# GpSimd's products with a convolution tap: tensor-scalar in place of tensor-tensor instructions

## The chip, the cores and the metric

The kernel runs on one core of a Trainium2 chip. The metric is the device time of one execution in microseconds (us). The engines are named as the profile names them: PE (TensorE's matmuls), PEld (its weight loads), DVE (VectorE), ACT (ScalarE), POOL (GpSimd) and SP (SyncE, which here only issues DMAs).

## The reference

A causal depthwise convolution of seven taps, whose taps are shared by the 24 channels of a head and made by a softmax over the taps, and then a feed-forward part with a product in the middle:

```python
w = softmax(weight)                       # [8 heads, 7 taps], float32
x_pad = 6 zero rows ahead of x            # x: [8, 3904, 192]
conv[b, s, h*24+g] = sum_k w[h, k] * x_pad[b, s+k, h*24+g]
a = conv @ w1                             # [31232, 192] @ [192, 1024]
b = conv @ w2
h = a * b @ w3                            # [1024, 1024]
out = h @ w_out                           # [1024, 192]
```

## The kernel before, in words

**The products.** w3 and w_out are multiplied once at the start (`W_sb`), so that each token needs `a`, `b`, their product and one more matmul. The tokens are two streams of 15616 (r = 0 and 1), cut into 31 rounds of 512 tokens (the last has 256); a round treats both streams. `first_product` (line 518) makes for each of eight blocks of 128 features the two factors with 64-row matmuls (L489), casts the one on ACT (L497) and multiplies it by the other on DVE (L508) into the tile `abT`. `second_product` (line 528) multiplies `abT` by `W_sb` (L540), copies to `osb` on ACT (L545) and stores it (L552).

**The groups.** Rounds go in groups of four (lines 721 to 750): the four first products, and then the eight second products. Group 0 is rounds 0 to 3. The schedule is by hand: `manual_schedule` keeps the order of the program on each engine, and each DMA queue (SP's, POOL's) goes in the order of issue.

**The convolution** must be done ahead of the rounds that use it. It is made in three ways:

- By TensorE with band matrices (`conv`, L398), for the first rounds and, in the groups 1 to 5, for the first two rounds of the second group after p (`load_alone`, `store_alone`).
- In the groups p = 1 to 6, `shared_head` (line 295) makes the last two rounds of the group after p (one short round for p = 6), eight heads on a tile `xv` with tokens along the partitions: 128 partitions with W = 8 tokens each (W = 2 for p = 6), both streams, in bf16. Heads 0 to 3 go to POOL, heads 4 to 7 to DVE. A head is W x 2 x 24 = 384 columns (96 for p = 6).
- DVE's four heads fuse multiplication and addition (L317, L320), with an accumulator in two PSUM banks that are held for the time (`held`); ACT makes their first product (L315).

**A head on POOL** is a first product into `acc` (L325), then for each of the six other taps a product into `term` (L328) and, but for the last, an addition to `acc` (L331); the last additions write bf16 into the tile `y` (L334). `acc`, `term` and the taps `wv` are float32, `xv` bf16. POOL's order in a group (lines 726 to 733) is: head 0; from p = 2 on the four loads of `load_alone` (L342); head 1; the two loads of the next `xv` (L279); heads 2 and 3; a small DMA of zeros where a sequence starts within the tile (L292). After the group's second products stands the store of `y` (L364, POOL's queue) to the array `rows` in DRAM, which waits for DVE's heads too, and on SP's queue the transposes (L471) that read `rows` into the ring `xT`, from which the first products read. The second products of group 1 and later are stored from SP's queue.

Of the kernel before, what the change touches and what calls it, by code (L numbers as in the profile page):

```python
# [11 lines left out]
ALU = mybir.AluOpType  # L12
# [4 lines left out]
def kernel(  # L17
# [14 lines left out]
    G = D // H  # L32
    DFF = moe_w1.shape[1]
    JT = DFF // 128
    PAD = K - 1

    NS = 2
# [144 lines left out]
    for p0 in (0, Q):  # L182
        nc.gpsimd.affine_select(
            out=diag[p0:p0 + Q], in_=ones[p0:p0 + Q].to_broadcast([Q, Q + PAD]),
# [25 lines left out]
    def warm(n):  # L210
# [14 lines left out]
        out=wall, in0=wall, in1=wmax.unsqueeze(2).to_broadcast([1, H, K]), op=ALU.subtract)  # L225
# [5 lines left out]
        out=wrow, in0=wall, in1=wsum.unsqueeze(2).to_broadcast([1, H, K]), op=ALU.mult)  # L231
# [38 lines left out]
    def share(v):  # L270
        R0, R1 = SHARED[v]
        t0, n = R0 * CH, min(R1 * CH, TS) - R0 * CH
        return t0, n // 128
# [21 lines left out]
    def shared_head(v, h, f):  # L295
        xv, y = shared[v]
        W = share(v)[1]
        if y is None:
            y = shared[v][1] = work.tile(
                [128, W, NP, NS, Q], BF16, tag="convo", bufs=2, name="y")  # L300
        on_vector = f is nc.vector
        if on_vector:
            acc = held[0][1][:, h % 2, 0:W * NS * G]
        else:
            acc = work.tile([128, W * NS * G], FP32, tag="acc", bufs=2, name="acc")
        flat = acc.rearrange("p (m g) -> p m g", g=G)
        by_row = acc.rearrange("p (s r g) -> p s r g", r=NS, g=G)
        tap = lambda k: wv[:, h, k:k + 1]
        xs = lambda k: xv[:, k:k + W].rearrange("p s r c -> p (s r) c")[:, :, h * G:h * G + G]
        parts, o = [], 0  # L310
        for k, c0, m in segments(h * G, G):
            parts += [(y[:, :, k, r, c0:c0 + m], r, slice(o, o + m)) for r in range(NS)]
            o += m
        if on_vector:
            nc.scalar.activation(out=flat, in_=xs(PAD), func=ACT.Copy, scale=tap(PAD))  # L315
            for k in range(PAD - 1, 0, -1):
                f.scalar_tensor_tensor(out=flat, in0=xs(k), scalar=tap(k), in1=flat,  # L317
                                       op0=ALU.mult, op1=ALU.add)
            for dst, r, cs in parts:
                f.scalar_tensor_tensor(  # L320
                    out=dst, in0=xv[:, 0:W, r, h * G + cs.start:h * G + cs.stop],
                    scalar=tap(0), in1=by_row[:, :, r, cs], op0=ALU.mult, op1=ALU.add)
            return
        wide = lambda k: tap(k).unsqueeze(2).to_broadcast([128, W * NS, G])
        f.tensor_tensor(out=flat, in0=xs(PAD), in1=wide(PAD), op=ALU.mult)  # L325
        for k in range(PAD - 1, -1, -1):
            term = work.tile([128, W * NS * G], FP32, tag="term", bufs=2, name="term")
            f.tensor_tensor(out=term.rearrange("p (m g) -> p m g", g=G), in0=xs(k),  # L328
                            in1=wide(k), op=ALU.mult)
            if k:  # L330
                f.tensor_tensor(out=acc, in0=acc, in1=term, op=ALU.add)  # L331
        term = term.rearrange("p (s r g) -> p s r g", r=NS, g=G)
        for dst, r, cs in parts:
            f.tensor_tensor(out=dst, in0=by_row[:, :, r, cs], in1=term[:, :, r, cs], op=ALU.add)  # L334
# [38 lines left out]
    def segments(c0, n):  # L373
        out = []
        while n:
            m = min(n, Q - c0 % Q)
            out.append((c0 // Q, c0 % Q, m))
            c0, n = c0 + m, n - m
        return out
# [302 lines left out]
    def put_rows(b, last):  # L682
# [7 lines left out]
        out=wv, in0=wv, in1=top.unsqueeze(2).to_broadcast([128, H, K]), op=ALU.subtract)  # L690
# [5 lines left out]
        out=wv, in0=wv, in1=top.unsqueeze(2).to_broadcast([128, H, K]), op=ALU.mult)  # L696
# [16 lines left out]
    for p in SHARED:  # L713
        for i, h in ((-1, 4), (-1, 5), (1, 6), (3, 7)):
            at.setdefault((p, i), []).append((shared_head, p, h, nc.vector))
# [5 lines left out]
    for p, rounds in enumerate(groups):  # L721
        if p == 1:
            load_alone(1)
            pad_shared(1)
        if p in SHARED:
            for h in range(0, 4):
                shared_head(p, h, nc.gpsimd)
                if h == 0 and p > 1 and p in ALONE:
                    load_alone(p)
                if h == 1 and p + 1 in SHARED:  # L730
                    load_shared(p + 1)
            if p + 1 in SHARED:
                pad_shared(p + 1)
        for j, R in enumerate(rounds if p else ()):
            first_product(R)
            if R + GROUP < NR and j < 2:
                transposes(R + GROUP)
        if p in SHARED:
            free.append(free.pop(0))
            held.append(banks())  # L740
            free.insert(0, free.pop())
            run(at.get((p, -1), ()))
        for i, (R, r) in enumerate((R, r) for R in rounds for r in range(NS)):
            second_product(R, r, R == NR - 1 and r == 1, nc.sync if p else nc.gpsimd)
            run(at.get((p, i), ()))
        if p in SHARED:
            drained(held.pop()[0])
            store_shared(p)
            for R in range(*SHARED[p]):
                transposes(R)  # L750
# [30 lines left out]
```

## Time and profile before

| | |
|---|---|
| median of 3 runs | 517.45 us (516.1 to 517.6) |
| profiled execution, its own time | 515.89 us |
| its span | 514.2 us |
| granted TensorE clock | 1.00 |
| POOL's products of 384 columns (L328 and L325) | 120 x 828 ns and 20 x 847 ns |

A row of the profile's groups gives the line, the engine, the operation, out<-in by tile names with partitions x elements and type, the count, and after the bar the busy time (us), the mean of one (ns), and the idle time of the engine just before it with what ended it. A row in order of time begins with start and length in us and ends with the idle time before it in square brackets. The page's slices are 40 equal parts of the span, about 12.9 us each, with the busy share in tenths. "Landing" is the time from a DMA's issue to its completion.

### The profile page before, as it was taken

The page shows a single profiled execution, that of the slowest core. Times are in us where ns is not written, and L with a number is a line of the kernel's source. Part 1 is how long each engine was busy: PE and PEld are TensorE (multiplying, and loading weights), DVE is VectorE, ACT ScalarE, POOL GpSimd, SP SyncE. Part 2 cuts the span into 40 slices and gives each one's busy share as a digit, 9 for nine tenths or more (in the row PEclk, how much of TensorE's full clock was granted, in tenths as well). Part 3 has the DMA queues.
Part 4 walks back from the last instruction along what each step waited for, and adds up shares of the span by engine and source line. Part 5 has one row for each costly group of instructions (what it writes and reads, how often), then busy time and mean ns, then how long its engine had stood idle before and what let it go on. Part 6 is the DMA issues. An engine that isn't in the chain of part 4 may idle for free.

```text
span 514.2 us, 13632 instructions
## 1 busy us (share of the span) xinstructions
PE 508.4 (99%) x5608; PEld 339.1 (66%) x5608; DVE 401.1 (78%) x471; ACT 353.1 (69%) x469; POOL 321.4 (63%) x447
## 2 busy tenths in 40 slices
PE   8999999999999999999999999999999999999997
PEld 4555798454894458945598445985459845498587
DVE  6778723899959999499994999949999499972970
ACT  6887645777657776577765777657776577744762
POOL 8601534299999999699984999749997491000000
PEclk9999999999999999999999999999999999999999
DMA  8989999992965992787728787288842851035004
GB/s 118 155 152 127 134 216 231 207 197 54 193 193 149 137 108 94 237 146 102 95 93 248 141 104 91 93 255 134 93 51 94 259 112 32 2 102 171 6 3 155
DMA packets 137410, 67.91 MB, mean 132 GB/s; under 512 B 98899, under 2 KB 135939, under 8 KB 137283
## 3 DMA queue, kind: packets, MB, share of 16 engines
q0 software_dynamic: 48096, 26.92, 36.4%
q1 hardware_dynamic: 89105, 40.01, 32.7%
q8 instruction: 44, 0.72, 0.6%
q14 instruction: 19, 0.16, 0.1%
q10 hardware_dynamic: 146, 0.10, 0.1%
HBM read 39.60 MB, written 36.56 MB: 148 GB/s over the span
## 4 chain that ended last, share of the span: by engine, by line
PE 96%; DVE 2%; ACT 1%; issue 0%; ACTq 0%; DVEq 0%
PE pairs L489 60%; PE pairs L540 32%; PE pairs L398 2%; DVE abT L508 1%; PE pairs L575 1%; ACT asb L497 1%; PE pairs L451 1%; PE pairs L213 1%; DVE cprod L254 0%; ACT convo L419 0%; DVE convo L584 0%; ACT xT L463 0%; PE pairs L263 0%; PE pairs L615 0%; ACT osb L545 0%
## 5 line engine op out<-in xcount | busy, mean ns | idle before, releaser
L508 DVE TENSOR_TENSOR abT<-asb,pairs 128x1024 bf16<-128x1024 bf16 (+1 forms) x245 | 298.2, 1217 | 69.5 <-ACT asb L497 53.0
L489 PE MATMUL pairs<-xT,wd 64*128 64x512 bf16 (+2 forms) x3000 | 319.8, 371 | 0.7 <-DVE abT L508 0.3
L497 ACT CAST asb<-pairs 128x1024 bf16<-128x1024 f32 (+1 forms) x245 | 247.1, 1009 | 67.7 <-PE pairs L489 67.4
L489 PEld LDWEIGHTS <-wd 64*128 64x128 bf16 x3000 | 160.7, 94 | 153.6 <-issue 1.5
L540 PE MATMUL pairs<-W_sb,abT 128*128 128x192 bf16 x1952 | 165.0, 246 | 0.0
L540 PEld LDWEIGHTS <-abT 128*128 128x128 bf16 x1952 | 159.9, 98 | 5.3 <-issue 5.1
L545 ACT COPY osb<-pairs 128x384 f32<-128x384 f32 x122 | 58.6, 480 | 83.4 <-PE pairs L540 82.6
L331 POOL TENSOR_TENSOR acc<-acc,term 128x384 f32<-128x384 f32 (+1 forms) x120 | 107.3, 894 | 9.4
L328 POOL TENSOR_TENSOR term<-xv,wv 128x384 f32<-128x384 bf16 (+1 forms) x144 | 107.7, 748 | 0.5 <-DMA xv<-zeros 0.5
L317 DVE SCALAR_TENSOR_TENSOR pairs<-xv,wv,pairs 128x384 f32<-128x384 bf16 (+1 forms) x120 | 68.7, 572 | 7.2 <-ACT pairs L315 3.4
L364 POOL DMA_DIRECT2D rows<-y x6 | 3.7, 614 | 70.2 <-DVE y L320 61.3
L334 POOL TENSOR_TENSOR y<-acc,term 128x192 bf16<-128x192 f32 (+5 forms) x60 | 26.5, 467 | 1.9
L419 ACT CAST convo<-pairs 128x864 bf16<-128x864 f32 (+9 forms) x49 | 26.5, 613 | 0.2
L325 POOL TENSOR_TENSOR acc<-xv,wv 128x384 f32<-128x384 bf16 (+1 forms) x24 | 18.3, 764 | 9.7 <-DMA xv<-in_x_dram 9.6
L419 DVE CAST convo<-pairs 128x960 bf16<-128x960 f32 (+4 forms) x10 | 8.2, 858 | 17.2 <-PE pairs L398 17.2
L320 DVE SCALAR_TENSOR_TENSOR y<-xv,wv,pairs 128x192 bf16<-128x192 bf16 (+5 forms) x60 | 18.0, 351 | 1.1
L126 POOL DMA_DIRECT2D xb<-in_x_dram x20 | 13.9, 715 | 4.1 <-DMA xb<-in_x_dram 2.3
L342 POOL DMA_DIRECT2D xb<-in_x_dram x20 | 15.1, 772 | 0.0
L552 POOL DMA_DIRECT2D out_dram<-osb x8 | 6.1, 763 | 12.3 <-ACT osb L545 9.3
L279 POOL DMA_DIRECT2D xv<-in_x_dram x12 | 13.0, 1087 | 0.0
L315 ACT ACTIVATE pairs<-xv,wv 128x384 f32<-128x384 bf16 (+1 forms) x24 | 12.8, 550 | 0.0
L442 POOL DMA_DIRECT2D rows<-convo x2 | 1.1, 544 | 18.1 <-ACT convo L419 18.1
(65 smaller groups left out, 86.9 us busy)
## 6 DMA issues: line engine op xcount, KB each, us to landing
out_dram<-osb SPq DMA_DIRECT2D x52, 384.0 KB
xv<-in_x_dram POOLq DMA_DIRECT2D x10, 672.0 KB, 9.7
xb<-in_x_dram POOLq DMA_DIRECT2D x20, 216.0 KB, 7.3
rows<-y POOLq DMA_DIRECT2D x5, 768.0 KB, 5.9
out_dram<-osb POOLq DMA_DIRECT2D x8, 384.0 KB, 5.2
w3rows<-in_moe_w_dram POOLq DMA_DIRECT2D x2, 1024.0 KB, 11.8
xb<-in_x_dram POOLq DMA_DIRECT2D x8, 240.0 KB, 8.0
rows<-convo SPq DMA_DIRECT2D x6, 288.0 KB
```

The costliest lines, as they stand in the source:

```text
L317: f.scalar_tensor_tensor(out=flat, in0=xs(k), scalar=tap(k), in1=flat, op0=ALU.mult, op1=ALU.add)
L320: f.scalar_tensor_tensor(out=dst, in0=xv[:, 0:W, r, h * G + cs.start:h * G + cs.stop], scalar=tap(0), in1=by_row[:, :, r, cs], op0=ALU.mul ...
L325: f.tensor_tensor(out=flat, in0=xs(PAD), in1=wide(PAD), op=ALU.mult)
L328: f.tensor_tensor(out=term.rearrange("p (m g) -> p m g", g=G), in0=xs(k), in1=wide(k), op=ALU.mult)
L331: f.tensor_tensor(out=acc, in0=acc, in1=term, op=ALU.add)
L334: f.tensor_tensor(out=dst, in0=by_row[:, :, r, cs], in1=term[:, :, r, cs], op=ALU.add)
L419: f[e % len(f)](out=dst, in_=part)
L489: nc.tensor.matmul(p[:, r, e * n:e * n + n], wd[i][rs, k, ft * 128:(ft + 1) * 128], xT[k][rs, r0 + c0:r0 + c1], start=(k == 0), stop=(k == ...
L497: nc.scalar.copy(out=asb, in_=pa)
L508: nc.vector.tensor_tensor(out=dst, in0=asb, in1=pb, op=ALU.mult)
L540: nc.tensor.matmul(ops[:, (g - g0) * D:(g - g0) * D + D], ab[:, jt, r, g * 128:(g + 1) * 128], W_sb[:, jt, :], start=(jt == 0), stop=(jt = ...
L545: f(out=osb[:, g0:g0 + per, :].rearrange("p g d -> p (g d)"), in_=ops[:, 0:per * D])
```

## The change

In `shared_head`, for the heads that POOL makes, each product with a tap becomes a tensor-scalar instruction. Before, the tap `wv[:, h, k]`, one float32 value in each partition, was broadcast along all columns and went in as a second tensor; now it is the scalar operand of its partition, read from the same place in SBUF. Inputs, outputs, types and shapes stay, as do the additions and the number of instructions: 7 products a head, 4 heads a group, 6 groups, 168 in all.

```diff
-        wide = lambda k: tap(k).unsqueeze(2).to_broadcast([128, W * NS, G])
-        f.tensor_tensor(out=flat, in0=xs(PAD), in1=wide(PAD), op=ALU.mult)
+        f.tensor_scalar(out=flat, in0=xs(PAD), scalar1=tap(PAD), scalar2=None, op0=ALU.mult)
         for k in range(PAD - 1, -1, -1):
             term = work.tile([128, W * NS * G], FP32, tag="term", bufs=2, name="term")
-            f.tensor_tensor(out=term.rearrange("p (m g) -> p m g", g=G), in0=xs(k),
-                            in1=wide(k), op=ALU.mult)
+            f.tensor_scalar(out=term.rearrange("p (m g) -> p m g", g=G), in0=xs(k),
+                            scalar1=tap(k), scalar2=None, op0=ALU.mult)
             if k:
                 f.tensor_tensor(out=acc, in0=acc, in1=term, op=ALU.add)
```

## The prediction

> **What bounds the kernel now.** I read the page from the top: span and busy times, then the slices, to see whether one engine is full all the time or several take turns.
>
> ```profile
> span 514.2 us, 13632 instructions
> PE 508.4 (99%) x5608; PEld 339.1 (66%) x5608; DVE 401.1 (78%) x471; ACT 353.1 (69%) x469; POOL 321.4 (63%) x447
> PE   8999999999999999999999999999999999999997
> POOL 8601534299999999699984999749997491000000
> ```
>
> PE is full in every slice but the first and the last, and only 514.2 - 508.4 = 5.8 us of the span are not matmul time. POOL is nearly full from slice 9 on, that is from about 100 us, and done after about slice 34. So there are two questions: can PE be made to end earlier, and how near is POOL to holding PE up? The busy times of the six stretches in which PE works on one group of four rounds answer the first; the columns are start:end, length, and busy time (with instructions) of each engine.
>
> ```profile
> core 0: us, PE busy (x) PEld busy (x) DVE busy (x) ACT busy (x) POOL busy (x), PEclk, DMA share, GB/s
> 88.81:152.78 63.97, 63.97 (x673) 42.15 (x672) 54.49 (x62) 45.15 (x58) 52.02 (x65) 1.00 0.96 174
> 152.78:216.76 63.98, 63.98 (x674) 42.16 (x674) 54.49 (x62) 45.15 (x58) 57.97 (x73) 1.00 0.73 137
> 216.76:280.73 63.97, 63.97 (x673) 42.19 (x673) 54.49 (x62) 45.15 (x58) 53.17 (x67) 1.00 0.70 136
> 344.70:408.68 63.98, 63.98 (x674) 42.14 (x674) 54.49 (x62) 45.15 (x58) 52.02 (x71) 1.00 0.65 125
> ```
>
> PE is busy for the whole of each stretch (63.97 of 63.97), at a granted clock of 1.00. POOL has 52 to 58 us of work in 64. The waits of PE are all told in three rows:
>
> ```profile
> PE pairs L213 <- DVE ones L159: 1.1, 1, 1.1
> PE pairs L451 <- DVE convo L584: 0.4, 1, 0.4
> PE pairs L489 <- DVE abT L508: 0.3, 2, 0.2
> ```
>
> They come to 1.8 us, all of kinds that belong to the first 40 us, before POOL's first product. **PE bounds the kernel, and nothing that POOL does makes it wait.** A gain on POOL has nothing to shorten; a loss on POOL costs nothing until it is larger than POOL's slack.
>
> **The change, part by part.** It replaces the products of the four heads that POOL computes in each of the groups 1 to 6: one first product (L325) and six more (L328) per head, 28 per group, 140 of 384 columns in groups 1 to 5 and 28 of 96 columns in group 6. The additions (L331, L334) stay. Set beside each other, the instruction lists of the two kernels agree on PE, DVE, ACT and SP one by one, waits included; on POOL only the kind of these 168 instructions differs, in the same places with the same waits. So no DMA moves in its queue, no wait is added, and one number is unknown: how long a tensor-scalar instruction with its scalar in SBUF takes on POOL. No such row is in the trace. These are POOL's rows by form (busy us, mean ns):
>
> ```profile
> L331 POOL TENSOR_TENSOR acc<-acc,term 128x384 f32<-128x384 f32 x100 | 99.6, 996 | 7.8
> L328 POOL TENSOR_TENSOR term<-xv,wv 128x384 f32<-128x384 bf16 x120 | 99.4, 828 | 0.5 <-DMA xv<-zeros 0.5
> L325 POOL TENSOR_TENSOR acc<-xv,wv 128x384 f32<-128x384 bf16 x20 | 16.9, 847 | 9.6 <-DMA xv<-in_x_dram 9.6
> L328 POOL TENSOR_TENSOR term<-xv,wv 128x96 f32<-128x96 bf16 x24 | 8.3, 346 | 0.0
> L197 POOL COPY wd<-wd 64x768 bf16<-64x768 bf16 x6 | 4.8, 840 | 0.8 <-DMA wd<-in_moe_w_dram 0.8
> L183 POOL TENSOR_SCALAR_AFFINE_SELECT diag<-ones 64x70 bf16<-64x70 bf16 x2 | 0.5, 264 | 0.1
> L665 POOL COPY pace<-w3T 1x2 bf16<-1x2 bf16 x1 | 0.2, 174 | 11.6 <-DMA w3T<-w3rows 11.6
> ```
>
> The product now takes (99.4 + 16.9) / 140 = 0.831 us at 384 columns. From 96 to 384 columns it grows by 828 - 346 = 482 ns, 1.67 ns a column. The instructions that read one tensor are the copies: 174 ns at 2 columns, 840 at 768, so (840 - 174) / 766 = 0.87 ns a column, and at 384 columns 174 + 0.87 x 382 = 506 ns. That is the **lower bound**. The only row with scalar arithmetic in its name is the affine select: 264 ns for 70 columns. If all of that grew with the columns, 264 / 70 x 384 = 1448 ns: the **upper bound**. A tensor-scalar product reads one tensor as the copy does, with one operation on each element, so I take the value near the copy's, about 0.5 us, and keep both ends.
>
> *At 0.5 us:* POOL loses 140 x (0.831 - 0.506) = 45 us of work in groups 1 to 5, and some more in group 6. What becomes of it is read from POOL's order of time: start, length, instruction, idle time before it. Rows of the store that ends each group, and the first product of all:
>
> ```profile
> 102.99 0.83 POOL L325 TENSOR_TENSOR acc<-xv,wv 128x384 f32<-128x384 bf16 x1 [9.56 <-DMA xv<-in_x_dram]
> 154.36 0.59 POOL L364 DMA_DIRECT2D rows<-y  x1
> 212.96 0.63 POOL L364 DMA_DIRECT2D rows<-y  x1 [3.53 <-DVE y L320]
> 276.93 0.59 POOL L364 DMA_DIRECT2D rows<-y  x1 [8.90 <-issue]
> 340.92 0.63 POOL L364 DMA_DIRECT2D rows<-y  x1 [9.47 <-DVE y L320]
> 404.87 0.63 POOL L364 DMA_DIRECT2D rows<-y  x1 [9.82 <-DVE y L320]
> ```
>
> From group 2 on POOL waits 3.5 to 9.8 us before this store, because DVE's heads of the same tile are ready last. A faster POOL waits longer at the same place: the 45 us become idle time. Only group 1's store, which POOL itself holds up, would go out a few us earlier, as early as DVE's half allows. Its reader is the third round of the next group, as follows, and that round isn't waiting. The loads of the next tile and of the rows for TensorE's own convolution, which stand between the heads, go out up to some 5 to 10 us earlier within the group; PE doesn't wait for any DMA now, so nothing is won by it either. **Gain: 0.** Nor does DVE win or lose from its neighbour: its product takes the same time beside a busy POOL (first row, 213 to 267 us) and after POOL's last product (second row, 470 to 510 us).
>
> ```profile
> L508 DVE TENSOR_TENSOR abT<-asb,pairs 128x1024 bf16<-128x1024 bf16 x32 | 39.1, 1222 | 8.6 <-ACT asb L497 6.3
> ...
> L508 DVE TENSOR_TENSOR abT<-asb,pairs 128x1024 bf16<-128x1024 bf16 x20 | 24.4, 1222 | 10.8 <-ACT asb L497 9.4
> ```
>
> **How much slower POOL may be before PE notices.** The store of group p is read back by transposes on SP for the third and fourth round of group p+1. The first two rows are PE's first factors of groups 2 and 6; the third is SP's transposes after group 1's store, three for each round; the fourth and fifth are the landing times (last number, us) of that store and of the smallest row store.
>
> ```profile
> 152.78 41.62 PE L489 MATMUL pairs<-xT,wd 64*128 64x512 bf16 x384
> ...
> 408.68 41.62 PE L489 MATMUL pairs<-xT,wd 64*128 64x512 bf16 x384
> ...
> 158.19 8.45 SPq L471 DMA_TRANSPOSE xT<-rows  x6
> ...
> rows<-y POOLq DMA_DIRECT2D x5, 768.0 KB, 5.9
> rows<-convo POOLq DMA_DIRECT2D x1, 36.0 KB, 2.0
> ```
>
> From store to the third round's data: 158.19 - 154.36 = 3.8 us until the transposes start, 8.45 / 2 = 4.2 for three of them, and their landing, which no row gives; I bound it by 2.0 and 5.9. Together 10.1 to 13.9 us. The third round of group 2 starts at 152.78 + 41.62 / 2 = 173.6, so group 1's store may slip by 19.2 less that, 5 to 9 us. After group 1, POOL can use up its later waits: without them, the five groups take 51.4 (154.36 - 102.99), 55.1 (212.96 - 154.36 - 3.53), 55.1, 54.5 and 54.1 us, in all 270.2, so group 5's store could go out at 373.2. Its reader starts at 408.68 + 20.8 = 429.5. Allowed slip: 429.5 - 373.2 less 10.1 to 13.9 = 42 to 46 us, taken as 44. With d the added time of one product, PE waits once 140 d exceeds 44: d = 0.31 us, **a product of 1.15 us**. (Group 1 alone gives 28 d above 5 to 9, that is 0.19 to 0.33.) From there the time grows by 140 d - 44 us, since POOL then sets the pace of five groups.
>
> **Sum.** At any duration from 0.5 to 1.15 us the change is worth 0: 515.89 us, the profiled execution's own time (its span and 1.7 us around it). The median of the runs shown is 517.45, 1.56 above; on that scale my forecast is 517.4, no change.
>
> **The rivals.**
>
> *Slower: POOL becomes the bound.* One mechanism: the products take more than 1.15 us, the store of group 1 or 2 is late, PE stands before the third round of each next group. For it: no row shows the instruction; the affine select costs 3.8 ns a column against 1.67 for the product it would replace; POOL has only about a seventh of each group free; and forms do differ on POOL (996 ns for the addition, 828 for the product, same columns). Against it: it must be 38% slower than an instruction that reads two tensors. At the upper bound d = 1.448 - 0.831 = 0.617, and 140 x 0.617 - 44 = 42 us: 558 on the profile's scale, 559.6 on the median's. Halfway, at 1.30 us, it is 140 x 0.469 - 44 = 22 us: 539.
>
> *Much slower: the new form decides something anew for each column.* Then no row bounds it, and the same formula runs on: 2 us a product gives 140 x 1.17 - 44 = 120 us, 637. Nothing in the trace speaks for it but the affine select, which does make a choice per column, and stays within the bound above. The Trainium skill, "GPSIMD Engine Reference", 3.1, says that data-dependent branching costs about 12 cycles an element; with the 1.2 GHz of its section 1 that would be 384 x 12 / 1.2 = 3.84 us a product as an estimate, and some 377 us more, about 895 us. By that rule alone the change would be a disaster; the trace has no row of such a rate.
>
> *Faster.* It would need PE to end earlier, and the stretches above leave it no idle time after POOL's first product. Only the scatter of the runs (516.1 to 517.6) could show it.
>
> *The change does nothing to POOL either.* If the instruction runs at the old 0.83 us, all stays as it is: the same 517.4.
>
> **How the numbers follow.** No change, by a POOL that is quicker or up to 1.15 us a product: 0.52. POOL as the bound within the rows' bound, 519 to 560: 0.29. Beyond 560: 0.15, of which the per-column choice of the skill's size is 0.04. Faster: 0.04. About 0.3%, 1.55 us, is what a measurement of this kernel can tell from no change. So: faster 0.04, same 0.52, slower 0.44. The likeliest case alone spans 515.9 to 519.0; the range must take in the upper bound of the unknown duration and is 515.5 to 560, which leaves out the 0.15 above it and a little below.
>
> **What would show it.** Right: the products at about 0.5 us in POOL's groups, longer waits of the store for DVE's half in all of groups 1 to 5, stretches of PE still 63.97 us long and full. Wrong: a product of over 1.15 us, no wait left before the store, PE's first factor waiting for a DMA into xT at the third round of a group, and stretches as long as POOL's work in them. If the product is slow and the time still stands, my slack was too small; if it is quick and the time moves, something other than POOL's work, such as the loads that now go out earlier, is at play.

## The result, and the profile after

The changed kernel takes 532.68 us (median of 4 runs, 531.48 to 534.0), the kernel before in the same comparison 516.78 (515.91 to 517.6). The ratio is **1.0303, with a 95% interval of 1.0271 to 1.0335: slower by 3%**. The profiled execution took 531.48 us. The lines of its page that answer to those shown of before (the program has one line less, so L489 is now L488, L328 is L327, L364 is L363):

```profile
span 529.8 us, 13632 instructions
PE 513.8 (97%) x5608; PEld 343.8 (65%) x5608; DVE 401.0 (76%) x471; ACT 353.2 (67%) x469; POOL 388.0 (73%) x447
PE   8999999999999899999999989999899998999997
POOL 8501625199999999999999999999999999900000
```

POOL has grown from 321.4 to 388.0 us and has lost its gaps: from slice 9 to slice 35 it is never less than nine tenths busy. PE now has slices of 8. DVE and ACT have the same work as before (401.0 and 353.2 us busy, against 401.1 and 353.1). Next, POOL's rows by form (busy us, mean ns):

```profile
L327 POOL TENSOR_SCALAR term<-xv,wv 128x384 f32<-128x384 bf16 x120 | 149.2, 1243 | 0.0
L330 POOL TENSOR_TENSOR acc<-acc,term 128x384 f32<-128x384 f32 x100 | 99.6, 996 | 8.3
L324 POOL TENSOR_SCALAR acc<-xv,wv 128x384 f32<-128x384 bf16 x20 | 25.3, 1263 | 10.9 <-DMA xv<-in_x_dram 10.7
L327 POOL TENSOR_SCALAR term<-xv,wv 128x96 f32<-128x96 bf16 x24 | 12.5, 521 | 0.0
```

The product went from 828 to **1243 ns**; the addition stayed at 996. From 96 to 384 columns it grows by 722 ns, 2.51 ns a column against 1.67 before. In order of time a head is the better measure: from the first product of head 0 to that of head 1 it was 115.06 - 102.99 = 12.07 us, and is now 119.22 - 104.06 = 15.16. That is 3.09 us for seven products, **0.441 us each**. Now POOL's stores of the tile, group by group, with the first product of all:

```profile
104.06 1.25 POOL L324 TENSOR_SCALAR acc<-xv,wv 128x384 f32<-128x384 bf16 x1 [10.69 <-DMA xv<-in_x_dram]
...
167.82 0.60 POOL L363 DMA_DIRECT2D rows<-y  x1
...
235.02 0.64 POOL L363 DMA_DIRECT2D rows<-y  x1 [0.30 <-POOL y L333]
...
302.46 0.59 POOL L363 DMA_DIRECT2D rows<-y  x1
...
369.67 0.64 POOL L363 DMA_DIRECT2D rows<-y  x1 [0.31 <-POOL y L333]
...
436.47 0.64 POOL L363 DMA_DIRECT2D rows<-y  x1 [0.30 <-POOL y L333]
```

Before, the stores of groups 2 to 5 came every 64 us and waited up to 9.8 us for DVE's half. Now those of groups 1 to 5 come every 67 us and wait for nothing but POOL's own last addition. What that does to PE stands in its waits and in its order of time, here group 6:

```profile
PE pairs L488 <- DMA xT<-rows: 10.4, 12, 1.7
```

```profile
421.31 20.89 PE L488 MATMUL pairs<-xT,wd 64*128 64x512 bf16 x192
442.76 0.39 PE L488 MATMUL pairs<-xT,wd 64*128 64x512 bf16 x2 [0.56 <-DMA xT<-rows]
444.81 0.39 PE L488 MATMUL pairs<-xT,wd 64*128 64x512 bf16 x2 [1.66 <-DMA xT<-rows]
445.43 20.46 PE L488 MATMUL pairs<-xT,wd 64*128 64x512 bf16 x188 [0.23 <-DMA xT<-rows]
```

PE goes through two rounds (192 matmuls), stops, does two matmuls at a time as the transposes for the third round land, and goes on. Each of the groups 2 to 6 has two or three such waits at this place, 12 in all, and it is the new wait that the slower rival named.

The sum closes along POOL. Before, its work from the first product to the store of group 5 was 270.2 us without waits; 140 x 0.441 = 61.8 us more make 332.0, and measured are 436.47 - 104.06 = 332.4. That work also starts 1.1 us later than before (104.06 against 102.99), since the tile's load came later. PE's last wait ends 9.0 us after that store. From there to the end it takes 529.8 - 445.43 = 84.4 us; before, from the same point (429.5) to the end, it was 84.7. So the span is POOL's chain and PE's unchanged rest.

### The profile page after: what moved, and what is told of

Read it like the earlier page. It is cut to its first block, busy times and chain, and to the rows that moved or that the text cites. A ratio compares the mean times of both kernels' runs of the same rounds, so it can differ in the third digit from the quotient of the medians.

```text
span 529.8 us, 13632 instructions
## 1 busy us (share of the span) xinstructions
PE 513.8 (97%) x5608; PEld 343.8 (65%) x5608; DVE 401.0 (76%) x471; ACT 353.2 (67%) x469; POOL 388.0 (73%) x447
## 4 chain that ended last, share of the span: by engine, by line
PE 94%; DMA 3%; DVE 1%; ACT 1%; issue 0%; SPq 0%; ACTq 0%
PE pairs L488 58%; PE pairs L539 31%; DMA xT<-rows 3%; PE pairs L397 2%; DVE abT L507 1%; PE pairs L574 1%; ACT asb L496 1%; PE pairs L213 1%; PE pairs L450 1%; PE pairs L263 0%; SPq L470 0%; ACT convo L418 0%; DVE convo L583 0%; ACT xT L462 0%; PE pairs L614 0%
## 5 line engine op out<-in xcount | busy, mean ns | idle before, releaser
L488 PE MATMUL pairs<-xT,wd 64*128 64x512 bf16 (+3 forms) x3000 | 325.0, 374 | 11.1 <-DMA xT<-rows 10.4
L488 PEld LDWEIGHTS <-wd 64*128 64x128 bf16 x3000 | 165.2, 94 | 164.7 <-issue 16.4
L327 POOL TENSOR_SCALAR term<-xv,wv 128x384 f32<-128x384 bf16 (+1 forms) x144 | 161.7, 1123 | 0.0
L324 POOL TENSOR_SCALAR acc<-xv,wv 128x384 f32<-128x384 bf16 (+1 forms) x24 | 27.4, 1140 | 11.0 <-DMA xv<-in_x_dram 10.7
L126 POOL DMA_DIRECT2D xb<-in_x_dram x20 | 13.9, 716 | 3.9 <-DMA xb<-in_x_dram 2.7
L363 POOL DMA_DIRECT2D rows<-y x6 | 3.8, 626 | 17.8 <-DVE y L320 16.9
```

The lines of the kernel that those rows point to most:

```text
L324: f.tensor_scalar(out=flat, in0=xs(PAD), scalar1=tap(PAD), scalar2=None, op0=ALU.mult)
L327: f.tensor_scalar(out=term.rearrange("p (m g) -> p m g", g=G), in0=xs(k), scalar1=tap(k), scalar2=None, op0=ALU.mult)
L488: nc.tensor.matmul(p[:, r, e * n:e * n + n], wd[i][rs, k, ft * 128:(ft + 1) * 128], xT[k][rs, r0 + c0:r0 + c1], start=(k == 0), stop=(k == ...
```

## The experiments

Theory 1 is the slower rival: POOL is late, and only the amount of its work beyond what it had free counts. Theory 2: the new form harms by itself, for example through other engines, whatever the slack. A second question is why the instruction is slow.

**A dose: four and six of the seven products.** In `dose4` the first product and those of the taps 5, 4 and 3 are tensor-scalar, in `dose6` all but that of tap 0 (there the list is 5, 4, 3, 2, 1).

```diff
+            if k in (5, 4, 3):
                 f.tensor_scalar(out=term..., in0=xs(k), scalar1=tap(k), scalar2=None, op0=ALU.mult)
+            else:
+                f.tensor_tensor(out=term..., in0=xs(k), in1=wide(k), op=ALU.mult)
```

> Of the seven products of a head on POOL, four as tensor-scalar (the first and those of taps 5, 4, 3), three as before. Theory 1, POOL is late: 80 products in groups 1 to 5 lengthen by 0.44 us each (start to start), 35 us, less than the 46 us that POOL had free: the time of before, within 0.2% of it, so about 517. Theory 2, each tensor-scalar instruction harms whatever the slack (by a port, or by its effect on other engines): four sevenths of the 16 us, about 526.

> Six of the seven products of a head on POOL as tensor-scalar, only that of tap 0 as before. Theory 1: 120 products by 0.44 us is 53 us, 7 us over the 46 us that were free: 523 to 524. Theory 2: six sevenths of the 16 us, about 530.5.

Measured: `dose4` 516.64 us beside 516.6 of before, ratio 1.0013 (0.999 to 1.0036); `dose6` 524.11, ratio 1.0135 (1.0112 to 1.0158). 80 slow products cost nothing, 120 cost 7.5 us, all 140 cost 15.9. That is a threshold, as theory 1 has it, and not a price for each instruction, and beyond it the 20 products from 120 to 140 cost 8.4 us, near 20 x 0.441 = 8.8. The waits of PE for the rows agree: no such row in `dose4`, 5.4 us in `dose6`:

```profile
PE pairs L493 <- DMA xT<-rows: 5.4, 7, 1.3
```

**The same amount of work without the new form.** `load` is the kernel before with four more tensor-tensor products a head.

```diff
         f.tensor_tensor(out=flat, in0=xs(PAD), in1=wide(PAD), op=ALU.mult)
+        for k in range(4):
+            f.tensor_tensor(out=spare..., in0=xs(k), in1=wide(k), op=ALU.mult)
```

> The kernel before with no tensor-scalar product, but with four further tensor-tensor products after the first product of each head on POOL, into a tile that nothing reads: at 0.79 us start to start, 3.2 us a head, 63 us in the groups 1 to 5, about what the change adds (62). Theory 1: 63 less 46, so about 17 us slower, 533 to 534. Theory 2: no change, 517.

Measured: 542.5 us, ratio 1.0496 (1.0474 to 1.0518). Theory 2 falls: without one tensor-scalar product the kernel is slower than the change made it. The size was off, 25.9 us against my 17, and most of that was my figure for the added products. Four of them take 3.50 us start to start (105.22 to 108.72), not 3.16:

```profile
105.22 3.54 POOL L328 TENSOR_TENSOR spare<-xv,wv 128x384 f32<-128x384 bf16 x4
108.72 0.83 POOL L332 TENSOR_TENSOR term<-xv,wv 128x384 f32<-128x384 bf16 x1
```

The 3.54 us of the four are 0.83 us of the last and three starts of 0.90; from the last to the first `term` it is 0.79 again. So my 0.79 holds here from one tile to another, and products into the same tile start 0.90 apart; why is not shown by any run. 20 x 3.50 = 70 us less 46 is 24. In the trace, POOL's work from the first product to group 5's store is 445.34 - 104.44 = 340.9 us, 70.7 more than before, and the span grows by 25.2 (539.4): PE's last wait ends 9.6 us after that store in place of 9.0. The rest up to 25.9 lies between the profiled run (541.06) and the median.

**A head less on POOL.** `three` is the changed kernel with head 3 on DVE.

```diff
-        for i, h in ((-1, 4), (-1, 5), (1, 6), (3, 7)):
+        for i, h in ((-1, 4), (-1, 5), (1, 6), (3, 7), (5, 3)):
...
-            for h in range(0, 4):
+            for h in range(0, 3):
```

> The changed kernel with three heads on POOL in each group in place of four; head 3 goes to DVE, after the sixth of the group's eight second products. Theory 1, POOL is late and nothing else is wrong: POOL loses some 15 us a group, far more than the 3 us a group by which it was late; DVE gets 4 us more in a group where it has 54.5 of 64. PE is full again: 516 to 517.5. Theory 2, the tensor-scalar form harms other engines: three quarters of the 16 us stay, about 528. A third outcome, 518 to 522, would mean that DVE's fifth head now holds up the store or the products of the next group.

Measured: 516.0 us beside 516.08, ratio 0.9997 (0.9982 to 1.0012), with 105 products of 384 columns still at 1.24 us. PE is full again, and DVE carries the fifth head (58.36 us busy against 54.49):

```profile
152.70:216.70 64.00, 64.00 (x674) 42.13 (x672) 58.36 (x70) 45.75 (x60) 51.78 (x55) 1.00 0.77 155
```

**Why the instruction is slow.** `forms` is the kernel before with further instructions on POOL after its last store, three of each form. The first of them, with a tap as `t1`, stands for all; the others vary the scalar, the input and the operation:

```diff
+    for j in range(3):
+        nc.gpsimd.tensor_scalar(out=o3, in0=s3, scalar1=t1, scalar2=None, op0=ALU.mult)
...
```

> The kernel before, with eleven further instructions on POOL, three times each, after its last store (about 465 us, when POOL has nothing more to do); their results are not used. 384 columns unless said otherwise. Theory A, the scalar pointer costs (it has to be read from SBUF first): with a constant in place of the tap the tensor-scalar product falls from 1.24 us to 0.5 to 0.8 us. Theory B, the input's layout or type costs (runs of 24 bf16 values, turned into float32): with a contiguous float32 input it falls to below 0.9 us, and a copy of the same strided bf16 input is slow as well, 1 us or more. Theory C, the form itself is slow, for each column: with constant or pointer, strided or contiguous, it stays at 1.2 us, at 192 columns it takes about 0.76 us (the 521 ns at 96 columns and 1243 at 384 give 280 ns and 2.51 ns a column), and the copy takes about 0.5 us. I expect C. The time of the whole stays at that of before, unless the added work ends after PE.

The time of the whole was 516.84 us in a single run, beside 516.6. The rows of the forms; `pin` is strided like `xv`, `pf` and `pb` are contiguous, and a row without `wv` has a constant:

```profile
L771 POOL TENSOR_SCALAR po<-pin,wv 128x384 f32<-128x384 bf16 x3 | 3.7, 1247 | 0.3
L789 POOL TENSOR_SCALAR po<-pin,wv 128x384 f32<-128x384 bf16 x3 | 3.7, 1243 | 0.3
L775 POOL TENSOR_SCALAR po<-pf,wv 128x384 f32<-128x384 f32 x3 | 3.7, 1242 | 0.3
L773 POOL TENSOR_SCALAR po<-pin 128x384 f32<-128x384 bf16 x3 | 3.5, 1169 | 0.3
L769 POOL TENSOR_TENSOR po<-pin,wv 128x384 f32<-128x384 bf16 x3 | 2.5, 829 | 0.2
L785 POOL TENSOR_SCALAR po<-pf,wv 128x192 f32<-128x192 f32 x3 | 2.3, 762 | 0.3
L787 POOL TENSOR_SCALAR po<-pin,wv 128x384 f32<-128x384 bf16 x3 | 2.0, 658 | 0.3
L781 POOL CAST po<-pin 128x384 f32<-128x384 bf16 x3 | 1.5, 505 | 0.1
```

Theory A falls: the constant (L773) saves 74 ns, not 500. Theory B falls: contiguous float32 (L775) takes 1242, and the copy of the strided input (L781) 505. C holds for the single operation: multiplying (L771) or adding (L789), it stays at 1.24 us, and at 192 columns it is 762 as expected. But one row breaks C as I had put it: L787 is the same instruction with a *second* operation, multiply and then add, and takes 658. So it isn't tensor-scalar as such that is slow. `forms2` asks what it is about the second operation, with pairs of operations, taps and constants; one of them:

```diff
+        nc.gpsimd.tensor_scalar(out=o3, in0=s3, scalar1=t1, scalar2=1.0, op0=ALU.mult, op1=ALU.mult)
...
```

> The kernel before with further instructions on POOL after its last store, three of each; their results are not used. In the first such run the tensor-scalar product stayed at 1.24 us whatever its input, and fell to 0.66 us when a second operation (add, with the tap as its scalar too) was set. Theory D, a second operation as such takes the instruction to another, quicker routine: then every pair (multiply and add, multiply and multiply, add and multiply), with pointers or constants, takes about 0.66 us, and the single one 1.24. Theory E, only multiply and add together is quick, as one step: then the pairs multiply and multiply, add and multiply take 1.24 us or more. Theory F, the second pointer is what counts: then multiply and add with a constant 0 as second scalar is slow. I expect E for the pairs and no difference between pointer and constant beyond 0.1 us. At 96 columns the quick form should take 0.25 to 0.35 us.

In these rows L769 is the single multiplication, L771 multiply and add with two taps, L773 the same with a constant 0 as the second scalar, L775 with two constants, L777 multiply and multiply by 1.0, L779 add and multiply, and L781 multiply and add with two taps at 96 columns of contiguous float32:

```profile
L769 POOL TENSOR_SCALAR po<-pin,wv 128x384 f32<-128x384 bf16 x3 | 3.7, 1247 | 0.2
...
L771 POOL TENSOR_SCALAR po<-pin,wv 128x384 f32<-128x384 bf16 x3 | 2.0, 657 | 0.3
L777 POOL TENSOR_SCALAR po<-pin,wv 128x384 f32<-128x384 bf16 x3 | 1.8, 586 | 0.3
L779 POOL TENSOR_SCALAR po<-pin,wv 128x384 f32<-128x384 bf16 x3 | 1.8, 584 | 0.3
L773 POOL TENSOR_SCALAR po<-pin,wv 128x384 f32<-128x384 bf16 x3 | 1.7, 582 | 0.3
L775 POOL TENSOR_SCALAR po<-pin 128x384 f32<-128x384 bf16 x3 | 1.5, 513 | 0.3
L781 POOL TENSOR_SCALAR po<-pf,wv 128x96 f32<-128x96 f32 x3 | 1.3, 417 | 0.3
```

(The whole took 518.66 us in a single run, beside 516.08; this run is for the rows.) My choice, E, falls, and D holds: any second operation of those tried takes the instruction to about half. F falls too, as the form with a constant 0 (L773) is quick. Each scalar from SBUF costs some 70 to 75 ns (657, 582, 513). At 96 columns the row has 417, more than the 0.35 us I allowed, with two taps. What the engine does differently inside is not shown by any run; that there are two rates, 2.51 ns a column for one operation and about (657 - 417) / 288 = 0.83 for two, is. (The two rows of that difference have different inputs; in `two`, below, the product with one tap and times 1.0 takes 344 ns at 96 columns and 585 at 384, 0.84 ns a column.)

**The quick form in its place.** `two` is the changed kernel with that second operation; `two_load` adds the four further products of `load` to it.

```diff
-... scalar1=tap(k), scalar2=None, op0=ALU.mult)
+... scalar1=tap(k), scalar2=1.0, op0=ALU.mult, op1=ALU.mult)
```

> The changed kernel, each product with a second operation that leaves the value as it is (times the constant 1). By the runs before, 0.58 us a product in place of 1.24, and 0.83 in the kernel before. POOL then has some 31 us less to do in groups 1 to 5 than in the kernel before. If POOL's lateness was all: PE full again, the time of before (516 to 517.5), and not less, since PE is the bound. If a quicker POOL helps or hurts something else: another time.

> The kernel with four further tensor-tensor products a head on POOL, which took 542.5, with the head's own seven products in the tensor-scalar form with a second operation. The further products add 70 us in groups 1 to 5 (0.875 start to start), the quick form takes 31 away: 39, less than the 46 that were free. If the quick form keeps its 0.58 us in the place of the change: 516 to 518. If it is quick only when nothing runs beside it, as after the last store: 525 or more.

Measured: `two` 516.1 us beside 516.58, ratio 0.9987 (0.9966 to 1.0008); `two_load` 517.61 beside 516.58, ratio 1.0001 (0.998 to 1.0023). First the products of `two`, then its wait before the store:

```profile
L327 POOL TENSOR_SCALAR term<-xv,wv 128x384 f32<-128x384 bf16 x120 | 70.3, 585 | 1.9 <-DMA xv<-zeros 1.9
```

```profile
POOL rows L363 <- DVE y L320: 82.3, 4, 37.9
```

The products keep their 585 ns beside the other engines' work. `two` differs from the changed kernel in the second operation alone, so the 1243 ns there don't come from the place or from the neighbours either. POOL's wait for DVE grows from 61.3 to 82.3 us, and a fifth wait before this store, which the profile puts down to "issue", from 8.9 to 14.9; group 1's store goes out 4.7 us earlier (149.71 against 154.36). Together these are some 32 us, near the 31 expected: what POOL gains becomes idle time, as the prediction had it for a quick product. `two_load` shows what it is worth where POOL is the bound: 542.5 without the quick form, 517.61 with it. These 25 us are all that the added products cost, since PE is the bound again. No version here beats the kernel before, and the stretches of PE in it show why: it has nothing left to gain from POOL.

## Why the prediction was wrong, step by step

- **PE bounds the kernel, and a quicker POOL brings nothing: right.** `dose4`, `three` and `two` take POOL from more to less work than before, and all stand at the time of before.
- **Only the duration of the product is unknown: right.** `load` and `two` show that nothing else of the new form moves the time of the kernel.
- **The duration, "near the copy's, about 0.5 us": this step failed.** Measured are 1.243 us, inside the bounds of 0.506 and 1.448 but at the other end. The reason given was that the instruction reads one tensor and does one operation, as the copy does. The copy of the same strided bf16 input takes 505 ns, and the tensor-scalar product 1242 to 1247 with each input tried, so the number of tensors read doesn't set its rate. No other row of before gave the duration either. The upper bound held by luck: the affine select's proportion, 3.77 ns a column, gives 362 ns at 96 columns, where the product takes 521; and at the affine select's own 70 columns (264 ns) the product would take about 456, estimated from the 280 ns and 2.51 ns a column of its rows.
- **The slack, 42 to 46 us, and the point of 1.15 us: right.** The change uses up 61.8 - 15.6 (the growth of the span) = 46.2 us. `dose6` gives 120 x 0.441 - 9.6 (its span is 523.8) = 43.3 by its profiled run, the slowest of its four, and 45.4 by the medians. One term was too large: from store to data it was 9.0 us in group 6, not 10.1 to 13.9.
- **The slower rival's mechanism and price: right.** Its formula, with 1.243 for the product, gives 140 x 0.412 - 44 = 13.7 us, 529.6 against a profiled 531.48. The addition is 0.441 from start to start, which makes 4.1 us more, and the slack 2.2 us larger; together they are the 1.9 us that are missing.
- **The price from the Trainium skill ("GPSIMD Engine Reference", 3.1), about 12 cycles an element for data-dependent branching, does not apply.** 2.51 ns a column are about 3.0 cycles, an estimate with the 1.2 GHz of section 1 of that page of the Trainium skill. The rule of section 4.1 there, that GpSimd with one input runs at roughly line rate, would have confirmed my value. It agrees with the copy (0.87 ns a column) and with the two-operation form (0.84), and the single operation, at three times that, does not follow it.
- **The chances.** Slower had 0.44 against 0.52 for no change. With a threshold at 1.15 us between bounds of 0.5 and 1.45 and no row of the instruction, the question was open; it went the way of the second case. The measured 532.68 us lie inside the range of 515.5 to 560 only because the range took in that case up to its upper bound; the forecast itself was 517.4.

## What to carry to other kernels

An engine off the critical path has a price list with a step in it: work out how much time it has free until its result is read, and turn the change into so much time per instruction; here the step was forecast at 0.31 us a product (46.2 / 140 = 0.33 by the runs), and the form costs 0.44 more from start to start. Don't price an unmeasured instruction on GpSimd by how many tensors it reads: put three of the form into idle time of the engine and read its row, which here cost no time that a single run could show (`forms`, 516.84 beside 516.6). If a GpSimd product with a scalar of each partition is wanted, a second operation that changes nothing (times 1.0) took it from 1243 to 585 ns, below the 828 of the tensor-tensor product with a broadcast.

## What the runs showed of the hardware beside that

After two of the new waits, those of groups 2 and 4, PE ran for some microseconds at a lower clock. Stretches of the changed kernel around group 2's wait and, in the last two rows, around group 6's (start:end, length, busy times; the last three numbers are the granted clock, the DMA share and GB/s):

```profile
173.60:177.00 3.40, 0.80 (x6) 0.21 (x5) 1.60 (x2) 0.42 (x1) 3.32 (x4) 1.00 0.35 79
177.00:180.00 3.00, 2.99 (x16) 1.32 (x17) 1.22 (x1) 1.07 (x2) 2.92 (x3) 0.56 0.51 115
180.00:183.00 3.00, 3.00 (x26) 1.50 (x24) 1.47 (x2) 1.97 (x2) 2.83 (x4) 0.88 0.45 101
183.00:199.00 16.00, 16.00 (x150) 8.70 (x146) 15.12 (x13) 12.60 (x13) 15.59 (x17) 1.00 0.72 89
...
442.00:445.43 3.43, 0.99 (x7) 0.21 (x5) 1.79 (x2) 0.61 (x1) 3.18 (x9) 1.00 0.39 87
445.43:450.00 4.57, 4.57 (x44) 2.50 (x45) 2.95 (x3) 3.29 (x4) 4.15 (x11) 1.00 0.50 112
```

In group 2 PE was busy for 0.80 of 3.40 us, in pieces, with no single wait over 1.14 us, and then the clock fell. In stretches of half a microsecond it is 0.83 from 177.0 to 177.5, 0.50 up to 180.5, 0.76 up to 181.0 and 1.00 from there, which comes to 3.4 us at half the clock. The Trainium skill, "TensorE: Matmul & The Clock Gate", part 1, has the clock halved after an idle window of about 3.4 us and restored after as long a busy one. The slow stretch agrees in depth and length. The 3.4 us before it were not wholly idle, so the window needn't be; and group 6 had almost the same pause (0.99 busy of 3.43) with no slow stretch behind it, which no run here explains.

The matmuls of the first factors after the wait (188 or 190) take 22.15 and 22.16 us in groups 2 and 4 and 20.46 or 20.47 in the groups 3, 5 and 6. So the slow stretches make some 3 us of the 5.4 by which PE's busy time grew (508.4 to 513.8); the rest is not explained here. They lengthen the span by little or nothing, since PE waits for POOL's rows once more in the next group: its waits there are 2.6, 2.5 and 2.5 us in the groups 2, 4 and 6, but only 1.2 and 1.6 in the groups 3 and 5, which follow a slow stretch. That last point is argued from the order of time and was not tried.
